# A decode step of attention and MLP on one core: w4 loaded in contiguous rows, the last gelu as one activation, and pairs of slots split earlier in the load queue

## Chip, cores and metric

The kernel runs on one core of a Trainium2 chip. The metric is the device time of one execution in microseconds. The five instruction queues of the core are TensorE (PE, with its weight loads PEld), VectorE (DVE), ScalarE (ACT), GpSimd (POOL) and SyncE (SP); transfers from memory run on 16 DMA engines.

## What is computed

Eight sequences (batch 8) take one decode step through the same two layers twice. Layer A is attention against a cache of 4096 positions (16 query heads, 8 key and value heads, head size 256), layer B an MLP with a gelu. The step has one position, so every shift along the sequence in layer B moves in zeros, the part with w1 and w2 adds nothing, and what remains of layer B is the MLP with w3 and w4.

```python
B, D, Hq, Hkv, Sk, Dh, F = 8, 448, 16, 8, 4096, 256, 1792
def A(x):                       # x: (B, 1, D), all bf16
    q = (x @ wq) by head
    p = softmax(q k_cache^T * Dh**-0.5)
    return (p v_cache) by head @ wo
def MLP(x1):                    # what is left of layer B at one position
    return x1 + gelu_tanh(layernorm(x1) @ w3) @ w4
for _ in range(2):
    x = x + A(layernorm(x))
    x = x + MLP(layernorm(x))
```

(Layer B takes the layernorm of x as its own input and adds it up inside; the second norm in MLP is layer B's inner one.) The caches have 2 x 134 MB; keys and values are the same in both passes.

## The kernel before

**Tiles.** A key or value head of one sequence is 4096 x 256 values, cut into four chunks of 128 partitions x 2048 values (512 KB). SBUF holds a slab of NSLOT = 31 slots of that size, and every key or value chunk that is loaded, transposed or kept stands in a slot. Heads go in four pairs, m = 0 to 3. Names say pass, sequence, pair, what, head of the pair and chunk: B2m2V02 is the second pass (letter B), sequence 2, pair 2, values, head 0, chunk 2. The letters A and B in such names are the two passes, not the layers.

**Keys** are transposed, most of them on VectorE (L961, two instructions a chunk, from a raw slot into a target slot), some on TensorE with a copy back by ScalarE (L879, L939). Scores are L949 and L970, in the wide form L998 with L1002 for halves. Values are multiplied in L1112 or L1138. Three of the four pairs of keys of a sequence are kept transposed from the first pass and used again in the second; a few of these chunks are parked in PSUM (park, unpark; L1243 copies them back) to free their slots for a while.

**Turn.** Between the first pass over sequence b and its second pass stands turn(b): output projection with wo (L1186), norm, w3 (project, L589 and L591), gelu (L599 to L604), w4 (down, L614), norm, and the next queries with wq (L703). While it runs, TensorE's order has value matmuls of the second pass of sequence b-1 between its steps, as their values land. In the end all eight sequences' last MLP is computed together for the rows of sequences 0 to 6 (end), and alone for sequence 7 (end1, which calls block with base above 0; turn calls block with base 0).

**Gelu** before (gelu): scale by the norm's factor (on VectorE, L676 for one sequence), square (L599), a cubic's inner part (L600), tanh on ScalarE (L602), and (tanh + 1) times the input (L604); w4's result is halved by the 0.5 in the last addition (L678). The norm's factor comes from a reciprocal square root worked out on VectorE in seven steps (L546 to L556).

**Order.** Plan.schedule is a list scheduler that runs when the kernel is built. It gives every operation of every engine a place by priority and by modelled costs, chooses slots, and sets what each transfer waits for; on the chip each engine follows its fixed order and waits on semaphores. All cache transfers are issued by SP in one order, so one that waits holds up those behind it. A transfer moves one, two or four chunks into as many adjacent slots. Where a pair is wanted and no pair of slots is free but a single one is, the scheduler may split the pair into two transfers; it does so only where its model of the queue has little left:

```python
if (len(us) == 2 and short and transfer < t + DRY and one is not None and slot_free[one][0] <= t + 1e-6
        and len(slot_free) > bool(raw or u.raw) + sum(1 for o in ready["act"] if o.target is not None)
        and free["sp"] <= t + 1e-6):
    order.insert(nxt[0] + 1, self.split(u, users))
```

Here transfer is the modelled end of all that is issued and DRY is in nanoseconds. The same model lets a transfer's first packet come 3300 ns after its issue at the earliest.

**Weights.** w3 and w4 are loaded once, after the first keys and values, on the same queue: w3 as three transfers of 128 rows (and a tail in two halves), w4 as one, with 14 rows of 448 values for each partition, 896 bytes each and 128 rows apart.

Of the kernel before, what the change touches and what calls it, by code (L numbers as in the profile page):

```python
# [3 lines left out]
P = 128  # L4
# [10 lines left out]
SLOT = 2048  # L15
AHEAD = (1, 2)
NT = 2
NS = 2
# [9 lines left out]
def BANK(layer, b, m, s):  # L28
# [5 lines left out]
    return 0  # L34
DRY = 2500.0
BLOCK, BLOCK_0, BLOCK_NS = 128, 84, 5500.0
# [10 lines left out]
class Op:  # L47
    __slots__ = ("eng", "emit", "cost", "deps", "prio", "idx", "on", "end", "turn", "name", "unit", "clock", "left", "long", "target", "n")

    def __init__(self, eng, emit, cost, prio, turn, name):  # L50
        self.eng, self.emit, self.cost, self.prio, self.turn, self.name = eng, emit, cost, prio, turn, name
        self.deps = {}
        self.idx = self.on = self.end = self.unit = self.clock = None
        self.left = 0
        self.long = False
        self.target = None
        self.n = 0


# [301 lines left out]
def bass_interleave_layers__gqa_block_cached__mixer_s_mlp__decode_kernel(  # L361
# [16 lines left out]
    ACT = mybir.ActivationFunctionType  # L378
    ALU = mybir.AluOpType
# [70 lines left out]
    U_wo = [rows(f"wo{i}", wo_sb[:, 8 * i:8 * i + 8, :].rearrange("p (h c) n -> p h (c n)", c=2), wo_src[:, 4 * i:4 * i + 4, :], P * 7168 * 1.05) for i in range(4)]  # L450
    U_w4 = [rows("w4", w4_sb[:, :, :], B_w4.rearrange("(t m) n -> m t n", m=P), P * 12544 * 1.1)]

# [127 lines left out]

    def project(w, wt, half, j0, j1, rhs, out0, nb, units, bufs, name, place=lambda j: j):


        def emit(e):
            last = None
            for j in range(j0, j1):
                o = psT[:, out0 + place(j) * nb:out0 + (place(j) + 1) * nb]
                for k in range(3):
                    e.matmul(o, w[:, k, j * P:(j + 1) * P], rhs(0, P, k), start=(k == 0), stop=False)  # L589
                i, k = (j, 4) if j < half else (j - half, 3)  # L590
                last = e.matmul(o, wt[:, i * P:(i + 1) * P], rhs(0, P, k), start=False, stop=True)  # L591
            return last
        add("pe", emit, (j1 - j0) * 4 * 27, bufs, [], [bT], units, name=name, n=4 * (j1 - j0))
# [61 lines left out]
    def block(b, n, last, base):  # L655


        x = xT[:, :, b]
        dve(lambda e: e.memset(syn, 0.0), 125, [], [Bs["yn"]], name=n + "c0")
        dve(lambda e: e.memset(sx1[64:128, 4:5], 0.0), 125, [], [Bs["x4"]], name=n + "c1")  # L660
# [15 lines left out]
        gelu(1, lambda: shf[:, :], lambda: sht[:, :], 16, [], n, 150, lambda e, o, i: e.tensor_single_scalar(o, i, sf[:, 2:3], ALU.mult), Bs["f"])  # L676
# [117 lines left out]
    def end():  # L794
# [663 lines left out]
```

## Time and profile before

| what | us |
|---|---|
| median of 3 runs (lowest, highest) | 1093.57 (1092.01, 1094.07) |
| the profiled execution, its own time | 1091.88 |
| its span, first to last instruction | 1090.1 |
| TensorE busy / its weight loads | 763.1 / 520.9 |
| VectorE busy | 833.7 |
| ScalarE busy | 212.5 |
| VectorE's transposes of keys, L961, 544 of them | 647.9 |
| moved by DMA | 448.96 MB, mean 412 GB/s |

Of the transfers of keys and values, 95 moved four chunks, 216 two and 20 one:

```profile
slots<-in_A_v_cache_dram SPq DMA_DIRECT2D x149, 1024.0 KB, 9.7
slots<-in_A_v_cache_dram SPq DMA_DIRECT2D x49, 2048.0 KB, 23.5
slots<-in_A_k_cache_dram SPq DMA_DIRECT2D x46, 2048.0 KB, 21.8
slots<-in_A_k_cache_dram SPq DMA_DIRECT2D x67, 1024.0 KB, 15.3
slots<-in_A_v_cache_dram SPq DMA_DIRECT2D x18, 512.0 KB, 8.9
...
w_sb<-in_B_w_dram SPq DMA_DIRECT2D x1, 1568.0 KB, 16.4
```

The columns are the tile and its source, the issuing queue, the count, the size, and the median time from issue to landing in us. The last line is w4.

How to read the other views: in tables of stretches each line has the stretch, its length, busy us and count for each engine, the granted TensorE clock, the busy share of the DMA engines and GB/s. In a timeline each line has start, duration, engine, source line, operation, tiles, and in brackets the idle time before it with what ended it. In a list of waits, total us, times and the longest follow.

### The profile page before, as it was taken

The page shows a single profiled execution, that of the slowest core. Times are in us where ns is not written, and L with a number is a line of the kernel's source. Part 1 is how long each engine was busy: PE and PEld are TensorE (multiplying, and loading weights), DVE is VectorE, ACT ScalarE, POOL GpSimd, SP SyncE. Part 2 cuts the span into 40 slices and gives each one's busy share as a digit, 9 for nine tenths or more (in the row PEclk, how much of TensorE's full clock was granted, in tenths as well). Part 3 has the DMA queues.
Part 4 walks back from the last instruction along what each step waited for, and adds up shares of the span by engine and source line. Part 5 has one row for each costly group of instructions (what it writes and reads, how often), then busy time and mean ns, then how long its engine had stood idle before and what let it go on. Part 6 is the DMA issues. An engine that isn't in the chain of part 4 may idle for free.

```text
span 1090.1 us, 33778 instructions
## 1 busy us (share of the span) xinstructions
PE 763.1 (70%) x15440; PEld 520.9 (48%) x15440; DVE 833.7 (76%) x1597; ACT 212.5 (19%) x323; POOL 72.1 (7%) x233
## 2 busy tenths in 40 slices
PE   3466596778677965768667786577766787667876
PEld 3255453465246533555325653365433654346545
DVE  5999559965996499955999469974799839996483
ACT  1022130213011311203112032121221221111300
POOL 0000000000000000000000010000100000000000
PEclk9995555556555565556656576565655565555656
DMA  9999999999999999999999999999999999999995
GB/s 358 406 421 419 410 418 428 421 411 416 428 423 406 411 427 426 422 396 422 427 426 418 399 424 427 427 418 400 424 427 425 412 406 426 425 424 408 408 423 230
DMA packets 52943, 448.96 MB, mean 412 GB/s; under 512 B 5552, under 2 KB 9536, under 8 KB 12608
## 3 DMA queue, kind: packets, MB, share of 16 engines
q1 hardware_dynamic: 52640, 446.42, 98.5%
q8 instruction: 121, 1.98, 0.7%
q10 hardware_dynamic: 160, 0.38, 0.1%
q14 instruction: 22, 0.18, 0.0%
HBM read 446.77 MB, written 0.01 MB: 410 GB/s over the span
## 4 chain that ended last, share of the span: by engine, by line
DMA 33%; DVE 33%; PE 21%; issue 6%; SPq 3%; ACT 3%; POOL 0%; POOLq 0%; DVEq 0%
DVE slots L961 26%; DMA slots<-in_A_k_cache_dram 24%; DMA slots<-in_A_v_cache_dram 9%; PE psV L1138 6%; PE psS L970 5%; SPq L434 3%; DVE pT L1068 2%; PE psS L949 2%; ACT slots L939 1%; PE psV L1112 1%; PE psT L614 1%; PE psT L703 1%; DVE slots L1151 1%; SPq L460 1%; PE psT L1186 1%
## 5 line engine op out<-in xcount | busy, mean ns | idle before, releaser
L961 DVE STREAM_TRANSPOSE slots<-slots 128x1024 bf16<-128x1024 bf16 x544 | 647.9, 1228 | 35.3 <-DMA slots<-in_A_k_cache_dram 26.8
L970 PE MATMUL psS<-qe,slots 128*128 128x8 bf16 x5760 | 224.6, 174 | 162.7 <-DVE slots L961 113.5
L970 PEld LDWEIGHTS psS<-qe,slots 128*128 128x128 bf16 x5760 | 190.5, 103 | 248.3 <-DVE slots L961 178.4
L1138 PE MATMUL psV<-slots,pT 128*8 128x512 bf16 x1528 | 182.7, 554 | 20.8 <-DMA slots<-in_A_v_cache_dram 14.7
L939 ACT COPY slots<-psK 128x1024 bf16<-128x1024 bf16 x80 | 78.4, 1015 | 166.9 <-PE psK L879 156.2
L879 PE MATMUL psK<-ident,slots 128*128 128x128 bf16 x640 | 74.0, 302 | 5.8 <-DMA slots<-in_A_k_cache_dram 5.6
L1032 POOL PARTITION_ALL_REDUCE small<-small x64 | 23.8, 373 | 720.1 <-DVE small L1030 463.3
L1149 ACT ACTIVATE slots<-psV 128x512 bf16<-128x512 f32 x48 | 28.8, 599 | 204.0 <-PE psV L1138 199.4
L879 PEld LDWEIGHTS psK<-ident,slots 128*128 128x128 bf16 x640 | 61.6, 140 | 10.7 <-DMA slots<-in_A_k_cache_dram 6.9
L998 PE MATMUL psS<-slots,qe 128*8 128x512 bf16 x232 | 54.2, 588 | 7.9 <-DVE slots L961 7.0
L1112 PE MATMUL psV<-pT,slots 128*128 128x2 bf16 x1568 | 50.9, 165 | 8.5 <-DMA slots<-in_A_v_cache_dram 8.3
L1138 PEld LDWEIGHTS psV<-slots,pT 128*8 128x8 bf16 x1528 | 31.3, 90 | 52.9 <-issue 21.0
L1112 PEld LDWEIGHTS psV<-pT,slots 128*128 128x128 bf16 x1568 | 47.4, 104 | 10.3 <-DMA slots<-in_A_v_cache_dram 8.1
L1068 DVE STREAM_TRANSPOSE pT<-psS 128x128 bf16<-128x128 bf16 x64 | 45.4, 709 | 5.6 <-PE psS L1060 3.0
L1053 ACT ACTIVATE pT<-psS 128x128 bf16<-128x128 f32 x56 | 15.6, 278 | 173.1 <-DVE psS L1050 173.0
L1151 DVE TENSOR_TENSOR slots<-psV,slots 128x512 bf16<-128x512 f32 x48 | 32.4, 675 | 19.0 <-ACT slots L1149 18.9
L1186 PE MATMUL psT<-small,wo_sb 128*128 128x1 bf16 x1024 | 34.9, 166 | 7.2 <-DVE small L1119 5.3
L1160 PE MATMUL psV<-same,slots 128*128 128x4 bf16 x320 | 14.3, 166 | 36.1 <-DVE slots L1151 30.5
L949 PE MATMUL psS<-qo,slots 128*128 128x2 bf16 x768 | 27.7, 166 | 13.8 <-ACT slots L939 10.7
L639 DVE TENSOR_TENSOR qe<-psT,small 128x32 bf16<-128x32 f32 x32 | 6.0, 189 | 40.2 <-PE psS L970 36.8
L1186 PEld LDWEIGHTS psT<-small,wo_sb 128*128 128x128 bf16 x1024 | 32.0, 104 | 9.3 <-DVE small L1119 6.6
L1119 DVE TENSOR_TENSOR small<-psV,small 128x4 bf16<-128x4 f32 x30 | 4.3, 145 | 39.5 <-PE psV L1112 39.5
(195 smaller groups left out, 762.7 us busy)
## 6 DMA issues: line engine op xcount, KB each, us to landing
slots<-in_A_v_cache_dram SPq DMA_DIRECT2D x149, 1024.0 KB, 9.7
slots<-in_A_v_cache_dram SPq DMA_DIRECT2D x49, 2048.0 KB, 23.5
slots<-in_A_k_cache_dram SPq DMA_DIRECT2D x46, 2048.0 KB, 21.8
slots<-in_A_k_cache_dram SPq DMA_DIRECT2D x67, 1024.0 KB, 15.3
slots<-in_A_v_cache_dram SPq DMA_DIRECT2D x18, 512.0 KB, 8.9
wo_sb<-in_A_wo_dram SPq DMA_DIRECT2D x4, 896.0 KB, 22.7
wq_sb<-in_A_wq_dram SPq DMA_DIRECT2D x3, 1024.0 KB, 11.3
w_sb<-in_B_w_dram SPq DMA_DIRECT2D x1, 1568.0 KB, 16.4
```

The lines of the kernel that those rows point to most:

```text
L434: return plan.load(Unit(u, lambda e, u_: e.dma_start(t, ap), nbytes, slotted=False))
L879: last = e.transpose(tile[:, j * P:(j + 1) * P], slots[u.slot][:, o:o + P], ident[:, :])
L939: return e.copy(slots[u.slot][:, 1024 * t:1024 * t + 1024], tile)
L949: last = e.matmul(o, slots[u.slot][:, i:i + P], q, start=(cc == 0), stop=(cc == 1))
L961: return e.transpose(o, i)
L970: last = e.matmul(o, slots[u.slot][:, i:i + P], qe[:, 128 * k + 64 * s + 8 * g:128 * k + 64 * s + 8 * g + 8], start=(g == 0), stop=(g == 7))
L998: last = e.matmul(o, q, K[:, lo:hi + 1:hi - lo, :, g, :], start=(g == 0), stop=(g == 7))
L1068: add("dve", lambda e: e.transpose(pZ[:, :, 0:3:2].rearrange("p n s r -> p n r s"), psS[x][:, 128:192].bitcast(bf).rearrange("p (n r s) -> ...
L1112: last = e.matmul(o, slots[u.slot][:, i:i + DH - cc:2], w, start=(c == 0 and cc == 0 and j == 0), stop=(c == NCH - 1 and cc == 1 and j == 7))
L1138: last = e.matmul(psV[x][32 * i:32 * i + 8, :].rearrange("p (k d) -> p k d", k=2), w, v, start=(s == 0 and c == 0), stop=(s == 1 and c == ...
L1151: add("dve", lambda e: e.tensor_tensor(part(1), psV[x][:, :], part(0), ALU.subtract), 590, [Bhalf[0]], [Bhalf[1]], [bV[x]], [v], prio=at - ...
L1186: last = e.matmul(psT[:, base + 4 * (2 * s + i) + c:base + 4 * (2 * s + i) + c + 1], wo_sb[:, a, d0:d0 + P], qo[:, a, b:b + 1] if base els ...
```

## The change

Three edits.

1. w4 is loaded by four transfers. Half h of its 1792 rows is cut into 512 and 384 rows; partition m takes four (or three) consecutive rows, 3584 (or 2688) bytes in one run. The hidden units of the MLP then stand in another order, and w3's columns are taken in that order: packed(i) gives every fourth (or third) column in place of 128 adjacent ones. This holds for all uses of w3 and w4.
2. In block with base above 0, which is the last MLP of sequence 7 alone, gelu is one ScalarE activation (Gelu_apprx_tanh) that reads w3's result from PSUM with the norm's factor as its scale. A dummy activation of one column that needs all exps of both passes done loads its table earlier. The last addition takes w4's result whole. The turns keep the gelu in steps (TURN_GELU is False).
3. DRY goes from 2500 to 3500.

```diff
+TURN_GELU = False
-DRY = 2500.0
+DRY = 3500.0
...
+        self.exp = name[0] in "AB" and name.endswith(("ex", "pn0", "pn1"))
...
-    U_w4 = [rows("w4", w4_sb[:, :, :], B_w4.rearrange("(t m) n -> m t n", m=P), P * 12544 * 1.1)]
+    w4_half = B_w4.rearrange("(h x) n -> h x n", h=2)
+    U_w4 = [rows(f"w4{h}{k}", w4_sb[:, 7 * h + 4 * k:7 * h + 4 + 3 * k, :].rearrange("p t n -> p (t n)"),
+                 w4_half[h, 512 * k:512 + 384 * k, :].rearrange("(m t) n -> m (t n)", m=P), P * 896 * (4 - k) * 1.03) for h in range(2) for k in range(2)]
...
+    def packed(i):
+        return slice(i, 512, 4) if i < 4 else slice(512 + i - 4, 896, 3)
-    def project(w, wt, half, j0, j1, rhs, out0, nb, units, bufs, name, place=lambda j: j):
+    def project(w, wt, half, j0, j1, rhs, out0, nb, units, bufs, name, place=lambda j: j, cols=lambda i: slice(i * P, (i + 1) * P)):
...
+                i, k4 = (j, 4) if j < half else (j - half, 3)
+                c = cols(i)
                 for k in range(3):
-                    e.matmul(o, w[:, k, j * P:(j + 1) * P], rhs(0, P, k), start=(k == 0), stop=False)
-                i, k = (j, 4) if j < half else (j - half, 3)
-                last = e.matmul(o, wt[:, i * P:(i + 1) * P], rhs(0, P, k), start=False, stop=True)
+                    e.matmul(o, w[:, k, (j - i) * P + c.start:(j - i) * P + c.stop:c.step], rhs(0, P, k), start=(k == 0), stop=False)
+                last = e.matmul(o, wt[:, c], rhs(0, P, k4), start=False, stop=True)
...
+        if base or TURN_GELU:
+            G = add("act", lambda e: e.activation(sht[:, 0:1], wgt[:, 0:1], ACT.Gelu_apprx_tanh), 1500, [Bwgt], [Bs["ht"]], name=n + "gt")
+            for o in plan.ops:
+                if o.eng == "act" and o.exp:
+                    G.deps[o] = False
...
-        project(w3_sb, w3t_sb, 7, 0, 14, rhs, 16, 1, U_w3 + w3_rest, [Bs["yn"]], n + "w3")
+        project(w3_sb, w3t_sb, 7, 0, 14, rhs, 16, 1, U_w3 + w3_rest, [Bs["yn"]], n + "w3", cols=packed)
...
-        gelu(1, lambda: shf[:, :], lambda: sht[:, :], 16, [], n, 150, lambda e, o, i: e.tensor_single_scalar(o, i, sf[:, 2:3], ALU.mult), Bs["f"])
+        whole = base or TURN_GELU
+        if whole:
+            add("act", lambda e: e.activation(sht[:, :], psT[:, 16:30], ACT.Gelu_apprx_tanh, scale=sf[:, 2:3]), 260,
+                [Bs["f"]], [Bs["ht"]], [bT], name=n + "ge")
...
+        else:
+            gelu(1, lambda: shf[:, :], lambda: sht[:, :], 16, [], n, 150, lambda e, o, i: e.tensor_single_scalar(o, i, sf[:, 2:3], ALU.mult), Bs["f"])
         down(1, lambda: sht[:, :], 32, [], n + "w4")
-        dve(lambda e: e.scalar_tensor_tensor(x[:, 0:4], psT[:, 32:36], 0.5, sxy[:, :], ALU.mult, ALU.add), 150,
+        dve(lambda e: e.scalar_tensor_tensor(x[:, 0:4], psT[:, 32:36], 1.0 if whole else 0.5, sxy[:, :], ALU.mult, ALU.add), 150,
...
-        project(w3_sb, w3t_sb, 7, 0, 14, rhs, 32, 8, U_w3 + w3_rest + u, [byn], "ew3")
+        project(w3_sb, w3t_sb, 7, 0, 14, rhs, 32, 8, U_w3 + w3_rest + u, [byn], "ew3", cols=packed)
```

More of the change, by code (lines that the diff above doesn't have):

```diff
@@ L47 @@
 class Op:
-    __slots__ = ("eng", "emit", "cost", "deps", "prio", "idx", "on", "end", "turn", "name", "unit", "clock", "left", "long", "target", "n")
+    __slots__ = ("eng", "emit", "cost", "deps", "prio", "idx", "on", "end", "turn", "name", "unit", "clock", "left", "long", "target", "n", "exp")
     def __init__(self, eng, emit, cost, prio, turn, name):
@@ L675, in block @@
             160, [Bs["xc"], Bs["f1"], Bs["x1"]], [Bs["xy"]], name=n + "xy")
-        gelu(1, lambda: shf[:, :], lambda: sht[:, :], 16, [], n, 150, lambda e, o, i: e.tensor_single_scalar(o, i, sf[:, 2:3], ALU.mult), Bs["f"])
+        whole = base or TURN_GELU
+        if whole:
+            add("act", lambda e: e.activation(sht[:, :], psT[:, 16:30], ACT.Gelu_apprx_tanh, scale=sf[:, 2:3]), 260,
+                [Bs["f"]], [Bs["ht"]], [bT], name=n + "ge")
+            if not base:
+                add("act", lambda e: e.activation(shf[:, 0:1], wgt[:, 0:1], ACT.Exp), 1500, [Bwgt], [Bs["hf"]], name=n + "gx").deps[plan.ops[-2]] = False
+        else:
+            gelu(1, lambda: shf[:, :], lambda: sht[:, :], 16, [], n, 150, lambda e, o, i: e.tensor_single_scalar(o, i, sf[:, 2:3], ALU.mult), Bs["f"])
         down(1, lambda: sht[:, :], 32, [], n + "w4")
-        dve(lambda e: e.scalar_tensor_tensor(x[:, 0:4], psT[:, 32:36], 0.5, sxy[:, :], ALU.mult, ALU.add), 150,
+        dve(lambda e: e.scalar_tensor_tensor(x[:, 0:4], psT[:, 32:36], 1.0 if whole else 0.5, sxy[:, :], ALU.mult, ALU.add), 150,
             [Bs["xy"]], [Bx[b]], [bT], name=n + "r2")
```

## The prediction, made before the changed kernel was run

> **What bounds the kernel now.** I read the page first (span, the DMA row, the queues), then the chain of waits, then the stretches around one turn, then the order of time at the end, and for single transfers the trace's packet records (start, size and duration of each packet) beside the start of each issue on SP.
>
> ```profile
> span 1090.1 us, 33778 instructions
> DMA  9999999999999999999999999999999999999995
> GB/s 358 406 421 419 410 418 428 421 411 416 428 423 406 411 427 426 422 396 422 427 426 418 399 424 427 427 418 400 424 427 425 412 406 426 425 424 408 408 423 230
> q1 hardware_dynamic: 52640, 446.42, 98.5%
> DMA 33%; DVE 33%; PE 21%; issue 6%; SPq 3%; ACT 3%; POOL 0%; POOLq 0%; DVEq 0%
> ```
>
> SP's queue keeps the 16 DMA engines busy for 98.5% of the span, so bytes bound the kernel, nearly. Two things are left. The GB/s row dips about every fifth slice, to between 396 and 411, where 418 to 428 is usual. And the last digit is 5: after the last bytes a tail runs with no transfer in it. The chain's shares (DMA and DVE 33% each) say that VectorE's transposes and the transfers take turns in being last.
>
> The dips are the turns. Mean rate, last column, around the turn of batch 3, in stretches of 5 us:
>
> ```profile
> 470.00:475.00 5.00, 2.92 (x81) 2.74 (x79) 2.23 (x3) 1.18 (x2) 0.00 (x0) 0.84 1.02 415
> 475.00:480.00 5.00, 2.40 (x72) 2.15 (x72) 4.09 (x10) 0.05 (x1) 0.37 (x1) 0.50 0.98 387
> 480.00:485.00 5.00, 4.06 (x106) 3.72 (x107) 1.35 (x5) 0.22 (x1) 0.84 (x3) 0.50 0.96 388
> 485.00:490.00 5.00, 3.95 (x103) 2.87 (x101) 1.18 (x8) 0.00 (x0) 0.36 (x1) 0.50 0.95 354
> 490.00:495.00 5.00, 4.42 (x116) 2.96 (x112) 2.67 (x21) 0.21 (x1) 0.03 (x1) 0.50 1.01 421
> 495.00:500.00 5.00, 4.96 (x54) 1.31 (x52) 2.33 (x12) 2.32 (x4) 0.40 (x1) 0.63 1.02 423
> 500.00:505.00 5.00, 4.78 (x135) 3.45 (x132) 1.05 (x5) 3.13 (x4) 0.00 (x0) 1.00 1.01 418
> ```
>
> Against 421 the second to fourth stretch lose (34+33+67)/421 x 5 = 1.6 us of transfer. Each of the turns of batches 2 to 7 loses 1.4 to 1.65 so. What is late there is the issue:
>
> ```profile
> SPq L460 <- PE psV L1112: 11.3, 5, 4.1
> ```
>
> In 476 to 488 us SP waits 11.3 us, five times, for value matmuls to free slots. Issues stand at 477.00, 478.12 and 481.28 (the two halves B2m2V00, V01), 483.81 (B2m2V02 and V03, a pair of slots), 485.58, 486.77. From an issue to its first packet, where the queue is empty, the packet records show 3.0 to 3.6 us (481.28 to 484.35, for one). The half issued at 481.28 is through at about 485.8; the pair issued at 483.81 can't begin before some 483.81 + 3.3 = 487.1. That hole of 1.3 us is most of the dip.
>
> **Part 1, gelu at the very end (four VectorE steps and a tanh become one ScalarE activation).** The end in order of time:
>
> ```profile
> 1084.40 0.23 DVE L676 TENSOR_SCALAR qe<-psT,small 128x14 bf16<-128x14 f32 x1
> 1084.67 0.17 DVE L599 TENSOR_TENSOR qe<-qe 128x14 f32<-128x14 bf16 x1
> 1084.89 0.17 DVE L600 SCALAR_TENSOR_TENSOR qe<-qe 128x14 f32<-128x14 f32 x1
> 1085.09 0.21 ACT L602 ACTIVATE qe<-qe 128x14 f32<-128x14 f32 x1 [13.21 <-DVE qe L600]
> 1085.34 0.17 DVE L604 SCALAR_TENSOR_TENSOR qe<-qe 128x14 bf16<-128x14 f32 x1 [0.28 <-ACT qe L602]
> 1085.57 1.57 PEld L614 LDWEIGHTS psT<-qe,w_sb 128*128 128x128 bf16 x56 [1.51 <-DVE qe L604]
> ```
>
> From the norm's factor (ready at 1084.35) to the down projection it is 1.22 us. After the change: 0.03 to reach ScalarE (1085.06 to 1085.09 here), the activation, 0.06 to TensorE. The activation is L602's 0.215 us and a per-partition scale read from memory, which these rows price at 0.09 (687 against 599 ns, same shape, the first with such an operand):
>
> ```profile
> L1149 ACT ACTIVATE slots<-psV 128x512 bf16<-128x512 f32 x48 | 28.8, 599 | 204.0 <-PE psV L1138 199.4
> L1038 ACT ACTIVATE slots<-psS,small 128x512 bf16<-128x512 f32 x8 | 5.5, 687 | 32.7 <-DVE small L1035 32.7
> ```
>
> So 1.22 becomes 0.40: **-0.82 us**, with nothing beside it to hide in. Its function's table has to be loaded once (1.283 us, the trace's one load); the built order puts load and a dummy activation right behind the last exp at 1065.16, so the copy L1048 (1065.62) starts at about 1066.7, 1.1 late, and behind it the transpose and L1068, needed first by the value matmuls at 1072.55. Cover is some 4 us; without it the 1.1 would be paid.
>
> **Part 2, w4 in four transfers of contiguous rows.** Before, 1792 packets of 896 B at 41 ns: 1792 x 41 / 16 = 4.59 us. After, 256 of 3584 B (141 ns, from the w3 rows) and 256 of 2688 B (estimate 110 ns, between 78 ns for 1792 B and 141): 4.02 us. **-0.56 us**, at about 115 us, where the values behind it wait 5.7 to 12.2 us from issue to first packet, so that the queue is full and the time counts.
> Its price is in project(): w3's 56 weight loads now read every third or fourth column. No row shows such a step; L1112 reads every second column at 104 ns a load, L970 adjacent ones at 103. I take nothing, as for L1112; the far end is twice the pace, 28 ns more for each of 56 loads. The Trainium skill's SBUF — State Buffer (the cacheline note under Door 1) says that bf16 strides of up to 8 elements stay free; no run here shows it yet.
>
> **Part 3, DRY 2500 to 3500.** Built, it makes nine more pairs into singles and one run of four into two pairs. Six of the pairs are B1m2V02 to B6m2V02, the very transfer behind the hole; three lie before 160 us. Split, V02 takes the slot that the parking transpose (TensorE, L879, to 482.52) frees, V03 the one of the next value matmul: issues at about 482.55 and 482.9, and the next pair at 483.81. The hole goes: 1.3 us in each of six turns. A split costs 16 packets of 159 ns for 8 of 311 on each engine and a semaphore packet of 9: 0.065 us.
> But is it kept? Further on in the same turn issues stand at 495.60, 498.34 and 500.62, each where a value matmul ends that the order of TensorE puts between turn steps (w4, q rows), and their first packets come 3.62, 3.35 and 3.57 us later: at the floor, no store left. The turn's steps hang on the last layer-A value piece, issued at 477.00, ahead of the split. The built orders of PE, DVE and ACT are unchanged there. So the stream, 1.25 us ahead at 490, is held to the old time by 501. What survives is the smallest margin over 3.35 among those issues, in turns 2 to 7: 0.1, 0.0, 0.5, 0.0, 0.5, 0.5 us. The third and fifth of these lead into periods in which VectorE's transposes do wait for K transfers (5.6 and 5.4 us in 608:738 and 869:1000), so I count 0.4 each; the last one runs into the end, where transfers are queued 7 to 17 us deep: 0.45. Bounds: 0 to 6 x 1.25 = 7.5. I take **-1.25**, and **+0.27** for the splits outside turns (three at 0.065, the four at 0.08).
> The Trainium skill's DMA: Bandwidth & Descriptors (Specifications) gives about 0.6 us to the first byte for transfers that SP issues. By that no hole was ever due to the issue, part 3 would only cost, and the sum would be that of (a) below. The packet records here, 3.0 us at least, don't agree.
>
> **Sum:** -0.82 - 0.56 - 1.25 + 0.27 = -2.4 us. The profiled execution took 1091.88 (span 1090.1 and 1.8 around it), so 1089.5 on its terms; it was 1.7 below the median of the runs, 1093.57, and from that **1091.2**.
>
> **Rivals.**
> (a) Nothing comes of the splits: turns decide, and all ten splits cost. -0.82 - 0.56 + 0.67 = -0.7: 1092.9. For it: the margins of 0.0. Against: the 0.5 in three turns.
> (b) The stream's lead is kept in all turns, since value matmuls that find data earlier also run earlier: -0.82 - 0.56 + 0.27 - 7.5 = -8.6: 1085. For it: 98.5% of queue share. Against: those matmuls aren't waiting for data (TensorE's waits for DMA in 477:505 sum to 0.2 us).
> (c) Slower: the strided weight loads run at twice the pace. w3 takes 56 x 28 ns = 1.6 us more in each of 8 turns and in the last block. The norm's root covers 0.5 of it in a turn (w3 ends 491.05, L676 starts 491.57), 0.26 at the end: +1.1 for each turn that decides its period, four to eight of them, +1.3 at the end, -2.4: +3.3 to +7.7, 1097 to 1101. It decides from about 10 ns more per load. Against it: L1112.
> (d) Slower by order: three splits before 160 us move instructions up to 345 us (value and score matmuls of the first turn trade places, 32 half score matmuls become 16 whole). If a turn step lands behind one value wait, 2.5 us (481.28 to 483.81) or two are lost: 1093.5 to 1096.5.
>
> **How the numbers follow.** The forecast has 0.49, (a) 0.22, (b) and what lies between 0.11, (c) 0.06, (d) 0.12. About 0.2% (2.2 us) is what runs of this kernel tell from no change: faster is below 1091.4, slower above 1095.8. The forecast's own spread is 1089.5 to 1092.8, most below 1091.4. Faster: 0.35 of the forecast, (b), little else: 0.47. Slower: (c), most of (d): 0.16. Same: 0.37. The range of 8 in 10 leaves out half of (b) and most of (c): 1087.0 to 1095.8.
>
> **What would show it.** Right: the last ScalarE activation followed by the down projection some 0.1 us on; no 896 B packets of w4; in 485:490 of a turn over 400 GB/s, and the dip come back, smaller, some 12 us later; periods between turns still near 130.9 us. Wrong: w3's 56 loads over 1.7 us; turns closer than 130 us (b); a longer stretch between 140 and 345 us (d); a second table load at the end.

## The result, and the profile after

The changed kernel takes 1094.62 us (median of 21 runs, 1092.99 to 1098.54) where the kernel before, on the same chip, takes 1093.18 (21 runs, 1092.01 to 1096.38). The ratio is 1.0016, with a 95% interval of 1.0010 to 1.0022: slower by about 1.7 us (1.4 by the two medians). The forecast was 1091.2, 2.4 us faster. The time lies inside its range and on the wrong side.

The page of the changed kernel, parts 1 to 4, the lines that answer to those of before:

```profile
span 1092.2 us, 33762 instructions
DMA  9999999999999999999999999999999999999996
GB/s 360 406 421 418 417 415 427 421 411 419 426 423 398 412 428 427 420 397 414 426 426 419 411 411 427 427 418 401 425 425 425 410 408 425 428 422 399 404 399 247
q1 hardware_dynamic: 52848, 446.42, 98.6%
DMA 39%; DVE 28%; PE 20%; issue 5%; SPq 3%; ACT 3%; POOL 0%; DVEq 0%; ACTq 0%
```

The queue is as full as before (98.6%), of a span that is 2.1 us longer. The dips of the turns are still there, and the four slices ahead of the last, 422 399 404 399, are lower than before (424 408 408 423).

The stretches around the turn of batch 3, the same 5 us windows as before (columns: busy time of PE, PEld, DVE, ACT and POOL, the granted clock, the DMA share, GB/s):

```profile
470.00:475.00 5.00, 2.64 (x71) 2.50 (x67) 1.35 (x2) 1.02 (x2) 0.00 (x0) 0.50 1.01 416
475.00:480.00 5.00, 2.74 (x80) 2.39 (x80) 4.17 (x10) 0.00 (x0) 0.37 (x1) 0.50 0.97 385
480.00:485.00 5.00, 3.72 (x94) 3.38 (x94) 1.43 (x5) 0.28 (x1) 0.84 (x3) 0.50 0.98 374
485.00:490.00 5.00, 3.89 (x98) 2.75 (x95) 1.35 (x9) 0.00 (x0) 0.32 (x1) 0.50 0.98 375
490.00:495.00 5.00, 4.69 (x124) 3.50 (x123) 2.60 (x20) 0.21 (x1) 0.08 (x1) 0.50 1.02 422
495.00:500.00 5.00, 4.99 (x52) 1.45 (x52) 2.29 (x12) 2.09 (x3) 0.40 (x1) 0.50 1.01 410
500.00:505.00 5.00, 4.77 (x122) 3.14 (x118) 1.27 (x7) 2.52 (x3) 0.00 (x0) 0.84 0.99 380
```

The stretch of the hole, 485 to 490, rises from 354 to 375 GB/s and not to over 400. Some 12 us later the dip is back: 410 and 380, where the kernel before had 423 and 418. Over the 35 us the sum of the last column is 2762 against 2806: this turn moves fewer bytes, not more.

The end, in order of time (start, duration, engine, line, operation, and in brackets the idle time before it and what ended it):

```profile
1087.04 0.15 DVE L561 SCALAR_TENSOR_TENSOR small<-small 128x1 f32<-128x1 f32 x1
...
1087.28 0.27 ACT L695 ACTIVATE qe<-psT,small 128x14 bf16<-128x14 f32 x1 [11.85 <-DVE small L561]
...
1087.61 1.49 PEld L624 LDWEIGHTS psT<-qe,w_sb 128*128 128x128 bf16 x53 [0.51 <-ACT qe L695]
```

The norm's factor is ready at 1087.19 and the down projection starts at 1087.61: 0.42 us, where it was 1.22. This part does what was forecast (0.40).

The last transfers before the end are another matter. SP's waits in 1040 to 1066 us, of the kernel before and then of the changed one (what ended them: total, times, longest):

```profile
SPq L460 <- PE psS L998: 9.8, 1, 9.8
SPq L460 <- DVE slots L961: 6.2, 1, 6.2
```

```profile
SPq L465 <- PE psV L1162: 12.8, 2, 10.9
SPq L465 <- DVE slots L985: 5.7, 1, 5.7
```

In the kernel before, the longest wait is that of B7m3V00, four chunks of values, for slots 8 to 11, and it ends with score matmuls of B7m0 (L998). In the changed kernel the plan has it in slots 16 to 19, and SP waits 10.9 us for value matmuls of B7m1 (L1162). The four single value pieces at the end of the stream then issue at 1062.5 to 1063.9 instead of 1057.1 to 1059.4. Of these 5 us, 2.3 were there before the last stretch began: the last layer-A value piece issues at 1002.27 in the changed kernel's trace, at 1000.00 in that of before. What the late issues do to the stream, before and after:

```profile
1050.00:1055.00 5.00, 5.00 (x83) 2.37 (x81) 4.95 (x16) 0.36 (x2) 1.27 (x4) 0.50 0.97 405
1055.00:1060.00 5.00, 4.32 (x42) 1.24 (x36) 5.00 (x12) 1.01 (x3) 0.00 (x0) 0.65 1.02 415
1060.00:1065.00 5.00, 4.67 (x92) 2.60 (x92) 3.55 (x20) 0.82 (x2) 0.37 (x1) 1.00 1.03 434
1065.00:1070.00 5.00, 3.84 (x101) 2.65 (x102) 2.29 (x6) 1.02 (x3) 0.52 (x2) 1.00 0.98 411
```

```profile
1050.00:1055.00 5.00, 2.68 (x33) 1.21 (x33) 2.41 (x7) 0.28 (x1) 0.37 (x1) 0.50 0.98 415
1055.00:1060.00 5.00, 5.00 (x75) 2.25 (x74) 4.95 (x16) 0.50 (x2) 0.96 (x3) 0.50 0.87 344
1060.00:1065.00 5.00, 3.67 (x48) 1.40 (x44) 4.90 (x17) 0.67 (x2) 0.00 (x0) 0.96 0.95 357
1065.00:1070.00 5.00, 4.58 (x119) 3.10 (x113) 2.17 (x11) 2.55 (x5) 0.37 (x1) 1.00 1.00 426
```

Against 420 GB/s the four windows lose (1680 - 1665)/420 x 5 = 0.2 us before and (1680 - 1542)/420 x 5 = 1.6 us after. So two places were to be told apart, the turns and the last stretch, and with them three parts of the change.

### The profile page after: what moved, and what is told of

It is laid out like the page before. It is cut to its first block, busy times and chain, and to the rows that moved or that the text cites. A ratio compares the mean times of both kernels' runs of the same rounds, so it can differ in the third digit from the quotient of the medians.

```text
span 1092.2 us, 33762 instructions
## 1 busy us (share of the span) xinstructions
PE 765.3 (70%) x15424; PEld 521.0 (48%) x15424; DVE 833.1 (76%) x1593; ACT 213.9 (20%) x325; POOL 72.4 (7%) x233
## 3 DMA queue, kind: packets, MB, share of 16 engines
q1 hardware_dynamic: 52848, 446.42, 98.6%
## 4 chain that ended last, share of the span: by engine, by line
DMA 39%; DVE 28%; PE 20%; issue 5%; SPq 3%; ACT 3%; POOL 0%; DVEq 0%; ACTq 0%
DMA slots<-in_A_k_cache_dram 26%; DVE slots L985 22%; DMA slots<-in_A_v_cache_dram 14%; PE psV L1162 5%; PE psS L994 5%; SPq L436 3%; PE psS L973 2%; DVE pT L1092 2%; PE psV L1136 1%; ACT slots L963 1%; PE psT L624 1%; PE psT L727 1%; ACT slots L1267 1%; SPq L465 1%; DVE slots L1175 1%
## 5 line engine op out<-in xcount | busy, mean ns | idle before, releaser
L1162 PE MATMUL psV<-slots,pT 128*8 128x512 bf16 x1528 | 183.5, 551 | 24.2 <-DMA slots<-in_A_v_cache_dram 16.1
L1162 PEld LDWEIGHTS psV<-slots,pT 128*8 128x8 bf16 x1528 | 31.7, 89 | 59.1 <-DMA slots<-in_A_v_cache_dram 22.3
L1136 PE MATMUL psV<-pT,slots 128*128 128x2 bf16 x1568 | 51.0, 165 | 8.8 <-DMA slots<-in_A_v_cache_dram 8.4
L1136 PEld LDWEIGHTS psV<-pT,slots 128*128 128x128 bf16 x1568 | 47.4, 104 | 10.9 <-DMA slots<-in_A_v_cache_dram 9.0
L973 PE MATMUL psS<-small,slots 128*128 128x2 bf16 x640 | 23.6, 166 | 20.3 <-issue 19.6
## 6 DMA issues: line engine op xcount, KB each, us to landing
slots<-in_A_v_cache_dram SPq DMA_DIRECT2D x141, 1024.0 KB, 10.9
```

What stands on the lines that cost most here:

```text
L973: last = e.matmul(o, slots[u.slot][:, i:i + P], q, start=(cc == 0), stop=(cc == 1))
L1136: last = e.matmul(o, slots[u.slot][:, i:i + DH - cc:2], w, start=(c == 0 and cc == 0 and j == 0), stop=(c == NCH - 1 and cc == 1 and j == 7))
L1162: last = e.matmul(psV[x][32 * i:32 * i + 8, :].rearrange("p (k d) -> p k d", k=2), w, v, start=(s == 0 and c == 0), stop=(s == 1 and c == ...
```

## The experiments

### The three parts, each alone

The changed kernel with the split condition put back, and the kernel before with one part each:

```
two_dry2500 (changed kernel):  -DRY = 3500.0        +DRY = 2500.0
dry_only    (kernel before):   -DRY = 2500.0        +DRY = 3500.0
w4_only     (kernel before):   +U_w4 in four transfers, w3's columns strided (cols=packed)
gelu_only   (kernel before):   +the table's dummy activation and the one gelu activation of the last block
```

> The changed kernel with DRY back at 2500: w4 in four transfers with w3's columns strided, and the last gelu as one activation. The changed kernel was 1.0016 of the one before (+1.4 us by the medians). Theory W (the strided weight loads, 31 ns apiece where they were 26.7 in the changed kernel's trace, lengthen each turn and eat more than w4 saves): still slower than before, +0.5 to +1.5 us, ratio 1.0005 to 1.0014. Theory S (the splits and the slots they lead to cost): faster than before by 0.8 to 1.4 us, ratio 0.9987 to 0.9993.

> The kernel before with DRY at 3500 and nothing else. Theory W: within 0.6 us of before, ratio 0.9995 to 1.0005. Theory S: slower by 2 to 3 us, ratio 1.002 to 1.003.

> The kernel before with w4 in four transfers and w3's columns strided, nothing else. Theory W: slower by 1 to 2.5 us, ratio 1.001 to 1.0023. Theory S: faster by 0.4 to 0.6 us, ratio 0.9995.

> The kernel before with the last gelu as one activation and nothing else. Both theories: faster by 0.7 to 0.9 us, ratio 0.9992; the span from the last value matmul (L1112) to the end 0.7 to 0.9 us shorter than the 10.1 us of before. If it isn't faster, the table load at 1065 us costs what the tail gains.

| kernel | median us | ratio to before, 95% interval |
|---|---|---|
| two_dry2500 | 1092.05 | 0.9990 (0.9981 to 0.9998) |
| dry_only | 1095.77 | 1.0025 (1.0016 to 1.0033) |
| w4_only | 1092.81 | 0.9999 (0.9991 to 1.0007) |
| gelu_only | 1092.19 | 0.9989 (0.9981 to 0.9998) |

Theory W (the strided weight loads) falls as the cause of the loss: without the splits the same kernel, strided loads included, is faster than before, and by its interval w4_only is at most 0.8 us slower. The split condition alone costs 2.7 us (1.7 to 3.6). The kernel two_dry2500 is faster than the kernel before and the changed one.

### Where the splits cost: early, in turns, at the end

The next three kernels have the 3500 ns in force for a part of the plan's time only. The condition reads in each (t in ns; the names are the pairs that become singles):

```
-transfer < t + DRY
+transfer < t + (3500.0 if t < 300e3 else DRY)             dry_early: A0m2V02, A2m0V00, B0m0K00
+transfer < t + (3500.0 if 300e3 < t < 1000e3 else DRY)    dry_turns2to6: B1m2V02 to B5m2V02
+transfer < t + (3500.0 if t > 1000e3 else DRY)            dry_turn7: B6m2V02
```

> The kernel before, with the 3500 ns in the split condition only for transfers planned in the first 300 us: three pairs (A0m2V02, A2m0V00, B0m0K00) become singles, no split in a turn. With 3500 ns everywhere, and nothing else changed, the time was 2.7 us over the kernel before. Theory 1 (the early order of value and score matmuls, rival (d) of the prediction, costs the time): 1.5 to 3 us slower than before, and the last layer-A value piece of the first turn issued over 1 us later than before. Theory 2 (each split in a turn costs some tenths, which add up from turn to turn): within 0.5 us of before. Theory 3 (the cost arises in the last stretch, where the planner meets other slots: B7m3V00 in slots that wait for value matmuls instead of transposes): depends on where this plan puts B7m3V00, here slots 16 to 19, as in the plan with 3500 everywhere: 1 to 1.5 us slower, with its issue 56 us or more behind the last layer-A value piece of the turn before it, and a gap of half a us or more in which no transfer runs around 1058 us.

> The kernel before, with 3500 ns only for transfers planned between 300 and 1000 us: five pairs (B1m2V02 to B5m2V02) become singles, each in a turn. Theory 1 (early order): within 0.5 us of before. Theory 2 (splits in turns add up): 1 to 2.5 us slower, and the last layer-A value piece of the last turn issued 1 to 1.5 us later than before. Theory 3 (last stretch): within 0.5 us of before, since here B7m3V00 stands in slots 8 to 11 as before, its issue about 55 us behind the last layer-A value piece. The prediction's own step (lead kept in turns 4 and 6 and given back in the others) would make it 0.8 us faster.

> The kernel before, with 3500 ns only for transfers planned after 1000 us: one pair (B6m2V02) becomes singles and one run of four in the last stretch may change its slots; B7m3V00 stands in slots 12 to 15. Theory 1 and Theory 2: within 0.4 us of before. Theory 3 (last stretch): if slots 12 to 15 are as late as 16 to 19, 1 to 1.5 us slower with a gap around 1058 us; if they are as early as 8 to 11, no difference. The prediction's own step: 0.4 us faster.

Measured: dry_early 1.0000 (0.9991 to 1.0009), dry_turns2to6 1.0007 (0.9998 to 1.0016), dry_turn7 1.0003 (0.9994 to 1.0012). Theory 1, the early order, falls: the kernel that has it takes the time of the kernel before. The three together make 1.1 of the 2.7 us, and none is told from nothing by itself. In dry_turn7 SP waits 10.4 us for value matmuls near the end, as in the changed kernel, and its 0.3 us (-0.7 to 1.3) fall short of the 1 to 1.5 that Theory 3 gave it, which the interval still allows in part. In dry_early B7m3V00 stands in slots 16 to 19, and nothing is lost: not the number of the slot counts, but what it waits for (there, transposes and scores of B7m0, as before).

### One split with the late ending, six without it

Which splits are made decides how the last stretch falls out. Two kernels, each on top of the kernel before and of two_dry2500, take the two apart:

```
+3500.0 if 820e3 < t < 950e3 else DRY       one_late, two_one_late: B5m2V02 only; B7m3V00 behind B7m1's value matmuls
+3500.0 if t < 430e3 or 690e3 < t < 950e3 else DRY
                                            six_early, two_six_early: six splits; B7m3V00 behind B7m0's transposes and scores
```

> The kernel before, with 3500 ns only for transfers planned from 820 to 950 us: a single pair, B5m2V02, becomes singles, one split instead of the nine of the changed kernel. By itself this moves the plan of the last stretch to the changed kernel's kind of ending: B7m3V00 stands in slots that come free behind value matmuls of B7m1 (kernel before: transposes of B7m0), and the last four value pieces in slots behind transposes of B7m0's own values. Theory E (the ending costs; splits elsewhere are worth their packets, 0.06 us each): about 1 us slower than before, ratio 1.0007 to 1.0012; the last value byte 80.2 us or more behind the issue of the turn's last layer-A value piece, where endings of the other kind have 79.3 to 79.9. Theory N (the number of splits costs, some 0.3 us each, by more packet time in the queue, wherever they stand): 0.3 us slower, ratio 1.0000 to 1.0005, queue time 1074.6 us against 1074.3.

> The kernel before, with 3500 ns for transfers planned in the first 300 us and in the windows of the turns that hold B1m2V02, B4m2V02 and B5m2V02: six of the nine splits, but the plan of the last stretch keeps the kind of ending of the kernel before (B7m3V00 behind transposes of B7m0, last value piece behind a value matmul of B7m1). Theory E: within 0.5 us of before (six splits at 0.06), last value byte 79.3 to 79.9 us behind the issue of the turn's last layer-A value piece. Theory N: six ninths of the 2.7 us that all nine cost, 1.8 us slower, ratio 1.0016, queue time 1076.3 us. The prediction's own step (lead kept in turn 6, a little in 4): 0.3 us faster or more.

> The changed kernel with 2500 ns (gelu and w4 alone, ratio 0.9990 when measured), and 3500 ns only from 820 to 950 us: one split, B5m2V02, and an ending of the changed kernel's kind. Theory E: about 1 us over the kernel with 2500 ns, so ratio 0.9996 to 1.0003 to the kernel before. Theory N: 0.3 us over it, ratio 0.9990 to 0.9995.

> The changed kernel with 3500 ns only in the first 300 us and in the windows of B1m2V02, B4m2V02 and B5m2V02: six of nine splits, and an ending of the kind of the kernel before. Theory E: within 0.5 us of the changed kernel with 2500 ns, ratio 0.9988 to 0.9995 to the kernel before. Theory N: 1.8 us over it, ratio 1.0005 or more.

| kernel | splits more | ratio to before, 95% interval |
|---|---|---|
| one_late | 1 | 1.0007 (0.9999 to 1.0016) |
| six_early | 6 | 1.0013 (1.0005 to 1.0022) |
| two_one_late | 1 | 0.9994 (0.9985 to 1.0002) |
| two_six_early | 6 | 0.9999 (0.9991 to 1.0008) |

(Splits are counted as transfers more than without the condition. The kernels with six also make one run of four into two pairs and join two pairs into a run of four.)

Theory E alone falls: six splits cost 1.4 us (0.5 to 2.4) with the ending of the kernel before. Theory N has the better of it here by the middles, though one_late costs more than one split at 0.3. A straight fit through ten kernels (dry_only, the three by time, the four above, two_dry2500 and the changed one) gives 0.22 us per split and -1.1 for the other two parts, with standard errors of about 0.04 and 0.3. The late ending comes out at 0.3 (0.25) when the late kernels are those of the second group below, and at 0.5 (0.2) when dry_turns2to6, whose B7m3V00 still waits for scores of B7m0, is counted with the first. Its share can't be settled by these times.

The traces show it more closely. From the packet records one can read when a given number of bytes had passed the queue. How late each run is against the run of before, in us, at the byte that before had moved at 1055 and at 1065 us:

```
                at 1055   at 1065   lost between
B7m3V00 and the last pieces wait as in the kernel before:
gelu_only          0.0       0.0       0.0
w4_only           -0.3       0.1       0.4
two_dry2500        3.3       3.6       0.3
dry_early          1.5       1.6       0.1
w4_adjacent        0.4       0.3      -0.1
six_early          0.6       0.6       0.0
two_six_early      1.6       2.3       0.7
one of them, or both, wait for B7m1's value matmuls or later:
one_late           1.9       2.5       0.6
two_one_late       0.5       1.0       0.5
dry_turn7          1.5       2.3       0.8
dry_turns2to6      1.3       2.2       0.9
dry_only           1.0       2.0       1.0
after              1.7       3.4       1.6
```

The first two columns of numbers hold a scatter of one to three microseconds between executions (two_dry2500's profiled one was slow from 250 us on, though its median is the second lowest up to here). In the last column the first group loses 0.0 to 0.7 us, the second 0.5 to 1.6: 0.2 and 0.9 in the mean, with an overlap. Counted on to the last value byte, some of the difference goes: 0.5 and 1.0 in the mean, and 1.2 both in the changed kernel and in two_dry2500. The marker named in the expectations, 80.2 us from the last layer-A value piece to the last byte, did not sort them (one_late 79.9, two_one_late 79.6, six_early 79.5, two_six_early 80.9), and the queue's time that Theory N gave was missed by one_late (1075.6 us for 1074.6) and nearly met by six_early (1075.8 for 1076.3). Whether the last stretch costs what the traces suggest needed a run of its own, the last one below.

### The price of a split, with the plan left alone

Here plan, slots, waits and order are those of the kernel before; chosen pairs are issued as two transfers of one slot, one behind the other, so that neither a lead nor another slot can come of it. And two kernels turn the condition further, to both sides:

```
cut_deep, cut_turn:
+if n == 2 and cut(u.name):
+    e.dma_start(<first slot>, <first chunk>).then_inc(u.sem, 16)
+    return e.dma_start(<second slot>, <second chunk>)
cut_deep: 56 pairs, A1..A7 m3K and m2V      cut_turn: B1m2V02 to B6m2V02
dry6000:  -DRY = 2500.0  +DRY = 6000.0      dry0:  -DRY = 2500.0  +DRY = 0.0
```

> The kernel before with its plan, slots, waits and order left as they are, but 56 pairs of slots (A1..A7, m3K00, K02, K10, K12 and m2V00, V02, V10, V12; in the kernel before they stand 5 to 21 us in the queue) issued as two transfers of one slot, one behind the other, on one semaphore. Theory P (a split is worth its packets, 0.065 us): 56 x 0.065 = 3.6 us slower, ratio 1.003. Theory T (a transfer of one slot holds the queue longer than half a pair: consecutive singles began 1.3 to 1.8 us apart in the traces, where half a pair is 1.26): 56 x 0.1 to 0.6, 6 to 34 us, 14 at 0.25, ratio 1.006 or more. Theory S (only plan and slots cost, not the transfer itself): 0 to 2 us.

> The kernel before with its plan left as it is, but the six pairs B1m2V02 to B6m2V02 issued as two transfers of one slot, both where the pair was, so that no lead comes of it. Theory P: 6 x 0.065 = 0.4 us slower at most, ratio 1.0000 to 1.0004. Theory T: 6 x 0.25 = 1.5 us, ratio 1.0014; nothing if the hole ahead of them hides it. Theory S: nothing.

> The kernel before with 6000 ns in the split condition: 430 transfers instead of 349 (359 with 3500). Theory P: 81 x 0.065 = 5.3 us slower, ratio 1.005. Theory T: 81 x 0.25 = 20 us, ratio 1.018. Theory S: scattered like the kernels with 3500, 1 to 4 us slower. The prediction's own reading, leads that fill holes: less than 5 us slower or faster.

> The kernel before with 0 ns in the split condition: 334 transfers instead of 349; no pair is split, the two singles B?m2V00, V01 of each turn among them. Theory P and the prediction's reading (a split in a turn fills a hole): the hole of a turn grows by the wait of the pair, slower by 1 us per turn or more, ratio 1.003 to 1.01. Theory T: 15 x 0.25 = 3.7 us faster, less what the lead of V00, V01 is worth. Theory S: within 2 us.

| kernel | splits against before | ratio, 95% interval | us per split |
|---|---|---|---|
| cut_deep | +56 | 1.0036 (1.0023 to 1.0049) | +0.07 (0.04 to 0.10) |
| cut_turn | +6 | 1.0013 (1.0004 to 1.0022) | +0.24 (0.07 to 0.40) |
| dry6000 | +81 | 1.0066 (1.0051 to 1.0080) | +0.09 |
| dry0 | -14 | 1.0107 (1.0087 to 1.0126) | 0.83 lost for each one taken away |

Where the queue is deep a split costs its packets, 0.07 us (Theory P; the forecast had 0.065), and Theory T falls there. dry6000's 0.09 a split, 7.2 us in all, lies a little above Theory P and far below Theory T; it also misses the prediction's own reading, less than 5 us. The queue's line of cut_deep shows what they are, 8064 packets more for the same bytes:

```profile
q1 hardware_dynamic: 60704, 446.42, 98.6%
```

In a turn the same cut, with no lead, costs 0.24 us, three times as much by its middle; the lower end of the interval is the deep queue's price. And dry0 shows that a split can be worth far more than it costs. Of its 14 transfers fewer, eight are two singles joined into a pair and six two pairs joined into a run of four. Its turns have the halves B?m2V00 and V01 in one transfer, which must wait for both slots. Its queue and its turn of batch 3 (which comes 5.4 us later than in the kernel before):

```profile
q1 hardware_dynamic: 50624, 446.42, 97.7%
```

```profile
483.00:488.00 5.00, 2.84 (x60) 2.49 (x61) 2.49 (x11) 0.28 (x1) 1.21 (x4) 0.50 0.93 383
488.00:493.00 5.00, 4.17 (x139) 3.84 (x135) 0.49 (x3) 0.00 (x0) 0.00 (x0) 0.50 0.80 272
493.00:498.00 5.00, 3.72 (x99) 2.71 (x100) 3.09 (x25) 0.21 (x1) 0.40 (x1) 0.50 0.99 382
```

272 GB/s: this hole is a real one. The packet records give the lead of the stream in the turns, as the mean time from the issue of the last layer-A value piece to the middle of three later transfers, over the turns of batches 2 to 7:

```
             B?m2V12   B?m3V12   next K10
before        16.01     26.05     39.63
gelu_only     15.98     26.05     39.61
after         15.50     25.91     39.59
cut_turn      16.15     26.22     39.79
dry0          16.69     27.70     41.26
```

gelu_only, which has the plan of before, repeats it to 0.03 us. The changed kernel is 0.5 us ahead some 16 us after the issue, 0.14 ahead at 26 us, and level at 40 us: in the mean the lead is given back whole. Single turns can't be read so closely, at 40 us they lie between 0.8 ahead and 0.9 behind. dry0 falls 1.6 us behind in each turn and stays behind: seven turns make 11.4 of its 11.7 us.

### w4's transfers and the strided columns

```
w4_adjacent (w4_only):  -project(w3_sb, ..., cols=packed)   +project(w3_sb, ...)    (both calls)
```

> The kernel before, with w4 in four transfers of contiguous rows, but w3's weight loads left at adjacent columns, so that the hidden units that meet the rows of w4 are others than the reference's. With strided columns the same kernel was 0.3 us faster than before at most (ratio 0.9999). Theory P (strided loads take back part of what the transfers bring, 0.22 us per turn where the norm's root does not cover them): 0.5 to 1 us faster than before. Theory Q (the strided loads are covered, and w4's bytes are worth 0.3 or less): 0 to 0.3 us faster. The prediction's step, 0.56 us, lies between.

Measured 0.9998 (0.9989 to 1.0007) beside w4_only's 0.9999 (0.9991 to 1.0007). P and Q can't be told apart in time. In the traces the price is plain. The weight loads of w3 in w4_adjacent, w4_only and the changed kernel (busy time, mean ns of one, idle before):

```profile
L600 PEld LDWEIGHTS psT<-qe,w_sb 128*128 128x128 bf16 x378 | 14.1, 104 | 5.5 <-DVE qe L572 3.9 <-issue 1.6
```

```profile
L600 PEld LDWEIGHTS psT<-qe,w_sb 128*128 128x128 bf16 x378 | 16.1, 113 | 5.5 <-DVE qe L572 3.9 <-issue 1.6
```

```profile
L600 PEld LDWEIGHTS psT<-qe,w_sb 128*128 128x128 bf16 x378 | 16.0, 112 | 5.4 <-DVE qe L572 3.8 <-issue 1.1 <-DVE small L574 0.4
```

A load of every third or fourth column takes 112 to 113 ns instead of 104; w3's block takes 1.70 us instead of 1.48, 0.22 us more per turn.

### The ending given back, with all splits kept

Behind 1050 us of the plan, a run of four slots is split into pairs whenever it is found late. On the changed kernel this keeps its splits in turns and takes away the wait for B7m1's value matmuls; on two_dry2500 it is the control.

```
after_end (changed kernel), two_end (two_dry2500):
-if short and len(us) == 4 and transfer < t + DRY4:
+if short and len(us) == 4 and transfer < t + (1e9 if t > 1050e3 else DRY4):
```

> The changed kernel, all its splits kept, with one more condition: behind 1050 us of the plan a run of four slots is split into pairs whenever the planner finds it late. So B7m3V00 and B7m3V10 become two pairs each, none of which waits for value matmuls of B7m1 ahead of the last ones. If the last stretch costs what the traces show (0.7 to 1.7 us): 0.7 to 1.5 us faster than the changed kernel, ratio 1.0003 to 1.0010 to the kernel before, and less than 0.4 us lost between the bytes of 1055 and 1065 us. If the splits alone cost (0.3 us each): as the changed kernel, 1.0016 or a little more.

> The same condition behind 1050 us on the changed kernel with 2500 ns, whose last stretch loses only 0.3 us in the trace: the control. If the condition only takes back what the ending loses: 0 to 0.3 us faster than without it, ratio 0.9987 to 0.9991. If it is as good in any plan (0.7 us or more): 0.9983 or less, and this is then the fastest kernel of the case.

| kernel | median us | ratio to before, 95% interval | without the condition |
|---|---|---|---|
| after_end | 1093.88 | 1.0000 (0.9990 to 1.0009) | 1.0016 (1.0010 to 1.0022) |
| two_end | 1091.54 | 0.9987 (0.9978 to 0.9996) | 0.9990 (0.9981 to 0.9998) |

By the ratios the condition takes 1.7 us from the changed kernel (the two intervals together leave 0.5 to 2.9), a little more than was expected, and 0.3 from the control (-1.0 to 1.6). By the medians it is 0.8 and 0.7. So the times show that the last stretch can be mended, but not that it cost the changed kernel more than the control; for that there are only the traces. SP's waits of after_end in 1040 to 1066 us:

```profile
SPq L465 <- PE psS L994: 9.5, 4, 4.5
SPq L465 <- DVE slots L985: 5.7, 1, 5.7
SPq L465 <- DVE wq_sb L551: 4.3, 1, 4.3
SPq L465 <- PE psV L1162: 2.3, 5, 0.7
```

The wait of 10.9 us for value matmuls is gone; five short ones of 2.3 us together are left. Its windows:

```profile
1050.00:1055.00 5.00, 3.03 (x45) 1.56 (x45) 2.76 (x7) 0.28 (x1) 0.37 (x1) 0.50 0.97 410
1055.00:1060.00 5.00, 5.00 (x66) 2.03 (x65) 4.95 (x16) 0.50 (x2) 0.96 (x3) 0.50 1.01 418
1060.00:1065.00 5.00, 4.10 (x54) 2.08 (x48) 4.64 (x18) 0.89 (x2) 0.00 (x0) 0.90 1.01 415
1065.00:1070.00 5.00, 4.60 (x124) 3.28 (x125) 2.33 (x12) 2.33 (x4) 0.47 (x2) 1.00 1.01 421
```

No window is below 410 GB/s: by the sum above the loss is 0.2 us, where the changed kernel loses 1.6. By the packet records after_end loses nothing between the bytes of 1055 and 1065 us (-0.1; under 0.4 was expected) and 0.4 to the last value byte, where the changed kernel loses 1.6 and 1.2. What is left between after_end and two_end, 0.0013 or 1.4 us (0 to 2.8), fits the price of the splits in cut_turn, 1.4. two_end has the lowest median of the case.

## Why the prediction was wrong

**Gelu at the end, -0.82: right.** 1.22 us became 0.42, 0.80 less, and alone the edit measures 1.2 us (0.2 to 2.1). The table's load put the copy behind it 0.96 us late (1.1 forecast) and its cover held: in gelu_only it is 8.23 us instead of 9.01 from the last value byte to the issue of the last output row. (That byte itself came at 1079.85 for 1079.51, less than the scatter of single executions.)

**w4, -0.56: not measurable, and its zero was wrong.** The packets came out as forecast (2688 B in 107.5 ns where 110 was estimated, 3584 B in 143). But the strided loads, counted at nothing, cost 4 ns each (1.48 to 1.70 us over 56). That is below the 10 ns from which rival (c) decides, and most of it lies beside the norm's root. The Trainium skill's SBUF — State Buffer (cacheline note under Door 1), by which such strides are free, doesn't agree with these rows: steps of three and four columns are not free, though the step of two of the value matmuls (L1136, 104 ns) is.

**The splits in turns, -1.25: the step that failed.** Two of its statements held. The lead is given back, and where it was said: the issues at 495.60, 498.34 and 500.62 stand at 496.02, 498.76 and 501.45 in the changed kernel, in the rhythm of the value matmuls, with first packets 3.3 to 3.4 us behind them. A split in a full queue costs 0.07.
What failed was sized from rows that don't carry it:
- The hole. The prediction said that "the pair issued at 483.81 can't begin before some 483.81 + 3.3 = 487.1", and it did begin. The pair's packets have 8 KB, those of the two halves ahead of it 4 KB, so the pair can be told by counting 8 KB packets. By 484.90 at the latest, 1.1 us behind the issue, its first one had started, and by 487.1 at least 41 of 128. In the turns of batches 1 to 7 the first has started 0.96 to 1.31 us behind the issue at the latest, and at least 26 to 58 of 128 have 3.3 us behind it. The floor of 3.0 to 3.6 us came from transfers that had others ahead of them: when the half of the example was issued (481.28), all 16 engines were busy, and they were so up to 482.5. Nor do the engines stop together: in the half microseconds from 484.5 to 486.5 there are 12.5 to 14.4 of 16 busy, never fewer. So there was no hole of 1.3 us to fill. The lead that the split bought was 0.5 us (16.01 to 15.50), not 1.25.
- "What survives". I counted 0.4 to 0.45 in three turns from margins of a single trace. 0.04 is what is left at 40 us in the mean, within what one trace repeats.
- The price in a turn. 0.065 a split was carried from the full queue to the turn, where cut_turn measures 0.24. Why it is more there isn't settled.

**What no step had: the last stretch.** The change's condition acts in turns, but the slots that the planner gives out afterwards shift, down to the last ones, where no turn follows that could take a delay back. In the changed kernel's trace 1.6 us of transfer are lost at 1050 to 1070 us (1.2 of them still at the last value byte), and 1.7 us (0.5 to 2.9) come back when only this stretch is mended (after_end). The prediction compared the orders of the engines around the turns, and took the end as "queued 7 to 17 us deep". The same list of slots, read to its end, would have shown other releasers.

**The sum, with the measured terms:** six splits in turns 1.4 (cut_turn), three others at 0.07, 0.2, and the last stretch 1.4 (1.7 less the 0.3 of the control): 3.0, where DRY alone measured 2.7 (1.7 to 3.6). With -1.2 for gelu and -0.1 for w4 that is +1.7; the changed kernel measured +1.7 (1.1 to 2.4). That it comes out so closely is luck: the term of the turns has an interval of 0.4 to 2.4, and that of the last stretch is at least as wide. What the times show is that the splits cost; that both places take part is shown by cut_turn for the turns, and for the last stretch by after_end together with the traces. How the cost divides between them stays open.

**The rivals.** (a), the splits are worth nothing, is what happened, with a price of 0.24 and not 0.065 in the turns. Its 1092.9 was too low by this and by the last stretch. (b) is out: nothing is kept. (c): its mechanism is real at 4 ns. (d), slower by order, 1093.5 to 1096.5, holds the time, but not for its reason: the early order by itself measures 1.0000 (0.9991 to 1.0009). A change of slots did cost, 900 us later.

The Trainium skill's DMA: Bandwidth & Descriptors (Specifications) has about 0.6 us to the first byte. The 1.0 to 1.3 us, at most, from the start of an issue to its first packet, of which the issuing instruction takes 0.33, are nearer to that than to the 3.0 us by which the prediction set the page aside. That no issue in a turn is worth moving does not follow from it: dry0 joins the issues of V00 and V01, 3.2 us apart in the kernel before, and loses 1.6 us per turn.

## What to carry to other kernels

A transfer that starts earlier gains only what its successors can keep. Follow the lead to the next issue that waits for compute, and count what is left there, not at the hole. A planner's threshold changes every choice after it: compare the plans up to the last transfer, above all behind the last point where a delay could be absorbed. Take the time from an issue to its first packet from a transfer that has nothing ahead of it, and identify its packets (here by their size) before a floor is built on it. To price a small edit, multiply it with everything else held still (56 cuts told 0.07 us each), and price it in the place where it will stand, since the same cut cost more in a nearly empty queue.

## What the runs showed of the hardware

- Singles of 512 KB in place of a pair of 1 MB cost 0.07 us in a queue 5 to 21 us deep, and 0.24 (0.07 to 0.40) in a turn, where the queue runs empty.
- When the queue starves, the 16 DMA engines fall apart in time. In 482.5 to 487.5 us of the kernel before the stall is 0.5 us of idle engines and another 0.4 us of packets that take longer than usual (8 KB in 398 to 776 ns, the mean of each half microsecond at the hole, against 311 ns). The DMA share alone shows too little of it: 0.95 in 485 to 490, where the rate is 354 GB/s and 421 is usual.
- In seven turns of the kernel before, the pair that SP issues when the queue runs empty has started its first packet 0.96 to 1.31 us behind the start of the issue, at the latest; of its 128 packets 8 to 20 can be told to have started after 2.4 us and 26 to 58 after 3.3.
- LDWEIGHTS of bf16 at column steps of three and four took 112 ns a record, at steps of one and two 104.
